# B, C and y of the last two batches turned in 32x32 squares on VectorE, in place of 128x128 transposes on TensorE

## The chip, the cores and the metric

The kernel runs on one core of a Trainium2 chip. The metric is the device time of one execution in microseconds (us). PE is TensorE, DVE is VectorE, ACT is ScalarE, POOL is GpSimd, and SP is the engine whose queue issues all transfers between the chip's main memory and SBUF (its on-chip memory). PSUM is where PE writes.

## The reference, cut to what matters

A scan with decay over sequences (4 batches, 8 heads, 768 tokens, head dimension 32, state dimension 16), followed by a mixer over tokens and channels with weights w1 (256x1024) and w2 (1024x256). All in fp32.

```python
# scan, chunk by chunk of 32 tokens, per batch and head
cum = cumsum(log(a));  L = exp(cum_i - cum_j) for i >= j, else 0
y = (C @ B.T * L) @ x  +  (C @ state) * exp(cum)
state = exp(sum(log a)) * state + sum_j B_j x_j * exp(cum_last - cum_j)

# mixer on x = y as (batch, 768 tokens, 256 channels)
h = x.T @ U @ V               # U (768, 32), V (32, 768)
u = x + h.T
out = u + relu(u @ w1) @ w2
```

## The kernel before

**Tiles.** A batch's 768 tokens are 6 blocks of 128; the scan works on pairs of blocks, so there are 12 pairs (pair k belongs to batch k // 3, place q = k % 3 in it). For pair k, `load_bc` and `load_x` bring B, C and x with tokens on partitions. `prep` multiplies B and C on DVE by the decay factors F, into the tile BC. `turning` makes the state dimension lie on partitions: four TensorE transposes with the identity (L478) into a PSUM bank "w", from which ACT copies T (B and C turned, L482) and Cm (C turned and masked by head, L488). `gram` (C B^T, L510), `mask` (DVE, tile M), `state` and `update` (the running state, DVE and POOL), `inter` (L630) and `intra` (L655) give y in two PSUM banks, channels on partitions. `yout` copies it to yT by ACT.

**From y to the mixer.** The mixer needs y with channels on partitions (yT), and with tokens on partitions (ytok). `ytokening` makes ytok from yT by four TensorE transposes a pair (L682) and one copy, by ACT in the first two batches and by DVE in the last two. `project` (x^T U) reads ytok, `parted` and `added` add h to yT, `split` makes three parts of u for exact products in three passes, `first`, `second`, `third` and `plain` are the product with w1 and the relu, `down` is the product with w2, to which ytok is added on DVE before it is stored. All these products are at L765.

**Order.** The kernel sets the order of all instructions itself, by a list of words, PLAN, which `follow` walks through. A word is a step and its indices: `B6` loads B and C of pair 6, `X6` its x, `w5` a piece of the weights, `c6` converts the words of a weight piece (loaded as 64-bit numbers) on DVE, ACT and POOL, `R` refines a weight. `P6` is `prep`, `T6` half of `turning` (each pair has it twice; `Q` and `V` are the same in smaller parts for the first pairs), `g6` `gram`, `m6` and `M6` the halves of `mask`, `s6`, `u6`, `i6`, `n6`, `j6`, `y6` state, update, inter, the two parts of intra, and `yout`, `t6` `ytokening`. With a batch first: `p`, `q`, `a`, `S` are `project`, `parted`, `added`, `split`; `f`, `e`, `h` and `U` are first, second, third and plain; `d` is a part of `down`. `F` and `E` put matmuls of the identity on PE, so and so many blocks of 128 columns, as fillers ahead of a step that waits.

Each engine runs its instructions in the order in which PLAN records them. Loads and stores all go through the SP queue in that order; a load word also waits for the DVE instruction recorded last before it. Every DVE instruction appears under L174, since a helper records them. `settled` is a small DVE copy for which the second part of `intra` waits. The pools: raw tiles "bc" and "x" have 4 buffers each, BC, T and Cm 3, PSUM two banks for each of the tags w, x, z and y.

Of the kernel before, what the change touches and what calls it, by code (L numbers as in the profile page):

```python
# [14 lines left out]
WCOLS = 512  # L15
NWORDS = 15
PLAIN = 2
TAGS = {(2, 1): "yyy", (3, 0): "yyy", (3, 1): "yyy"}


# [11 lines left out]


PLAN = (
    'YB0 F2 A1 YB1 Q0.2 A0 Q0.0 Q0.1 YX0 K0 YB2 YV0 F5 V0.0.0 V0.1.1 F1 g0 Q1.2 Q1.1 s0 V1.1.2 YX1 '
    'Q1.0 V1.0.2 m0 M0 n0 YX2 F3 g1 Q2.0 Q2.2 u0 YU0 M1 Q2.1 i0 j0 y0 s1 F1 V2.0.2 m1 n1 w0 u1 '
    'V2.1.3 c0 c0 c0 E3 i1 g2 m2 YB3 w1 M2 E4 j1 y1 s2 B5 v0 O0.0 w4 u2 c2 t1 i2 P3 X3 c2 B4 w2 c2 '
    'n2 j2 T3 c1 c1 y2 T3 O2.1 X4 p0 P5 g3 m3 M3 q0 T5 T5 n3 a0.1 a0.0 B6 c1 s3 U0.1.0 P4 w3 U0.1.1 '
    'u3 T4 T4 U0.0.1 i3 c5 c5 c3 g4 X5 j3 c5 c3 w5 s4 U0.0.0 m4 R3 U0.1.6 c3 y3 U0.1.2 P6 U0.0.6 M4 '
    'T6 u4 T6 B7 i4 g5 c4 c4 n4 w6 s5 j4 y4 R1 M5 U0.0.7 c4 U0.1.3 m5 U0.1.7 U0.0.5 R3 c6 u5 U0.0.3 '  # L40
    'P7 T7 w8 n5 R0 i5 c7 R2 X6 c6 g6 w7 j5 c6 y5 T7 U0.1.5 t5 M6 U0.0.2 X9 B10 c7 t3 m6 R2 t4 R1 '
    'c8 U0.0.4 c8 p1 U0.1.4 c7 B8 q1 R4 X7 c8 d0.0.2.0 c9 d0.0.1.0 c9 d0.0.1.1 c9 d0.0.2.1 d0.0.2.2 '
    'd0.0.2.3 d0.1.0.0 a1.0 d0.1.0.1 P8 d0.1.0.2 S1.0 a1.1 R7 d0.0.1.2 d0.0.1.3 d0.1.0.3 s6 g7 m7 '
    'M7 n6 R0 f1.0.0 u6 R6 f1.0.1 f1.0.4 e1.0.0 h1.0.0 f1.0.5 e1.0.4 e1.0.1 f1.0.6 h1.0.4 i6 s7 j6 '
    'h1.0.1 d0.0.0.0 e1.0.5 R4 h1.0.5 f1.0.7 X8 e1.0.6 h1.0.6 d0.0.0.1 d0.0.0.2 e1.0.7 h1.0.7 '
    'f1.0.3 R5 f1.0.2 B9 u7 d0.1.1.0 X10 d0.0.0.3 P10 e1.0.2 R5 y6 h1.0.2 S1.1 e1.0.3 d0.1.2.0 '
    'd0.1.1.1 d0.1.1.2 h1.0.3 d0.1.2.1 d0.1.2.2 T8 T8 d0.1.2.3 d0.1.1.3 n7 s8 u8 i7 g8 j7 P9 s9 '
    'f1.1.0 m8 y7 R7 f1.1.1 d1.0.1.0 M8 e1.1.0 u9 d1.0.0.0 i8 n8 h1.1.0 s10 j8 d1.0.1.1 d1.0.1.2 R6 '
    'd1.0.1.3 R4 R5 u10 d1.0.0.1 d1.0.0.2 d1.0.1.4 e1.1.1 d1.0.0.3 R7 d1.0.2.0 R6 d1.0.2.1 d1.0.2.2 '
    'B11 d1.0.2.3 d1.0.0.4 d1.0.0.5 d1.0.1.5 d1.0.2.4 T10 h1.1.1 f1.1.6 f1.1.7 d1.0.2.5 e1.1.6 '  # L50
    'e1.1.7 f1.1.2 h1.1.6 h1.1.7 f1.1.3 f1.1.4 f1.1.5 X11 e1.1.2 e1.1.4 h1.1.2 h1.1.4 e1.1.3 h1.1.3 '
    'e1.1.5 P11 h1.1.5 T9 T9 d1.1.0.0 d1.1.0.1 d1.1.2.0 d1.1.2.1 d1.1.0.2 d1.1.2.2 d1.1.0.3 y8 t6 '
    'd1.1.2.3 d1.1.1.0 d1.1.1.1 d1.1.1.2 d1.1.1.3 d1.1.2.4 d1.1.0.4 d1.1.0.5 t7 d1.1.1.4 d1.1.1.5 '
    'd1.1.2.5 T10 t8 g9 p2 m9 M9 i9 g10 m10 q2 T11 T11 M10 n9 a2.0 s11 u11 j9 g11 i10 n10 y9 m11 '
    'S2.0 M11 t9 f2.0.0 f2.0.4 f2.0.1 e2.0.0 h2.0.0 e2.0.4 f2.0.5 e2.0.1 h2.0.4 h2.0.1 f2.0.6 '
    'e2.0.5 h2.0.5 f2.0.2 f2.0.3 j10 y10 e2.0.2 e2.0.3 f2.0.7 h2.0.2 h2.0.3 i11 n11 a2.1 e2.0.6 '
    'e2.0.7 j11 h2.0.6 d2.0.0.0 S2.1 y11 d2.0.1.0 d2.0.1.1 d2.0.0.1 f2.1.0 h2.0.7 d2.0.1.2 t11 t10 '
    'e2.1.0 h2.1.0 d2.0.1.3 d2.0.0.2 d2.0.0.3 f2.1.2 d2.0.1.4 d2.0.0.4 d2.0.0.5 d2.0.1.5 f2.1.3 '
    'd2.0.2.0 e2.1.2 h2.1.2 e2.1.3 d2.0.2.1 p3 d2.0.2.2 f2.1.1 f2.1.4 h2.1.3 d2.0.2.3 e2.1.1 f2.1.5 '
    'h2.1.1 e2.1.4 h2.1.4 d2.0.2.4 e2.1.5 q3 d2.0.2.5 h2.1.5 f2.1.6 f2.1.7 a3.0 e2.1.6 e2.1.7 '  # L60
    'h2.1.6 d2.1.2.0 d2.1.2.1 a3.1 d2.1.0.0 d2.1.0.1 d2.1.2.2 d2.1.0.2 S3.0 f3.0.3 f3.0.2 h2.1.7 '
    'd2.1.2.3 d2.1.0.3 f3.0.1 e3.0.2 h3.0.2 d2.1.0.4 e3.0.3 d2.1.0.5 h3.0.3 f3.0.0 e3.0.1 d2.1.1.0 '
    'd2.1.1.1 d2.1.1.2 e3.0.0 h3.0.0 f3.0.5 f3.0.4 d2.1.1.3 f3.0.6 e3.0.4 d2.1.2.4 e3.0.5 h3.0.1 '
    'f3.0.7 h3.0.4 d2.1.2.5 d2.1.1.4 e3.0.6 e3.0.7 d2.1.1.5 d3.0.2.0 d3.0.2.1 h3.0.6 d3.0.2.2 '
    'd3.0.0.0 d3.0.0.1 d3.0.0.2 S3.1 f3.1.0 f3.1.4 f3.1.5 h3.0.7 h3.0.5 d3.0.2.3 e3.1.0 f3.1.1 '
    'h3.1.0 d3.0.0.3 e3.1.4 f3.1.2 e3.1.5 d3.0.0.4 d3.0.0.5 d3.0.2.4 d3.0.2.5 d3.0.1.0 h3.1.4 '
    'd3.0.1.1 h3.1.5 e3.1.1 f3.1.6 f3.1.3 h3.1.1 d3.0.1.2 e3.1.2 e3.1.3 d3.0.1.3 h3.1.2 h3.1.3 '
    'f3.1.7 e3.1.6 h3.1.6 d3.0.1.4 d3.0.1.5 e3.1.7 d3.1.2.0 d3.1.2.1 h3.1.7 d3.1.2.2 d3.1.2.3 '
    'd3.1.1.0 d3.1.1.1 d3.1.2.4 d3.1.2.5 d3.1.1.2 d3.1.1.3 d3.1.0.0 d3.1.0.1 d3.1.0.2 d3.1.0.3 '
    'd3.1.1.4 d3.1.1.5 d3.1.0.4 d3.1.0.5 ')  # L70


@with_exitstack
def kernel(
# [42 lines left out]
    Q = 32  # L117
# [71 lines left out]
            "g r s -> r g s"))  # L189

    x_sb, bc_sb = {}, {}
    pairs = [(b, q) for b in range(NB) for q in range(NPR)]

    def hold(load, until):
# [10 lines left out]

    def load_bc(k, blocks=(0, 1)):
        b, q = pairs[k]
        if k not in bc_sb:
            bc_sb[k] = raw.tile([P, NH, 2, 2, N], FP32, tag="bc", name="bc")
        for c in blocks:  # L210
            begin(
                out=bc_sb[k][:, :, 0, c],
                in_=B[b, :, ts(2 * q + c, P), :].rearrange("h s n -> s h n"))
            if c == 0:
                begin(
                    out=bc_sb[k][:, :, 1].rearrange("p h t n -> p h (t n)"),
                    in_=C[b, :, ts(q, 2 * P), :].rearrange("h (p t) n -> p h (t n)", t=2))

    def load_x(k, blocks=(0, 1)):
        b, q = pairs[k]  # L220
# [70 lines left out]
            load_words(n + 1, w2c(n - NQ - 1, FP32), w22[m * P:(m + 2) * P].rearrange(  # L291
                "(m p) d -> p m d", p=P))

    loads = dict(B=load_bc, X=load_x, w=load_w)
    early = dict(loads, V=lambda n: load_v(), U=lambda n: load_u())

    ident = const.tile([P, P], FP32)
# [55 lines left out]
                            axis=mybir.AxisListType.X, op=ALU.add)  # L353

    F = const.tile([P, NB, NPR, NH, 2, 2], FP32)
    kept = const.tile([P, NB, 2 * NC - 1], FP32)
    own2 = const.tile([P, NB, 2 * NC - 1, 2], FP32)

# [6 lines left out]
    def decays(bs, tag="w", which=range(2)):  # L365

        n = bs.stop - bs.start
        for i in which:
            d = bank(tag, n * NPR * NH * 2)
            view = d.rearrange("p (g h c) -> p c g h", g=n * NPR, h=NH)  # L370
            logs = la[:, bs].rearrange("p b (q c) h -> p c (b q) h", q=NPR)
            if i == 0:
                nc.tensor.matmul(out=view, lhsT=ref, rhs=logs, start=True, stop=True,
                                 skip_group_check=True)
            for c in range(2 if i else 0):
                for t in range(2):
                    nc.tensor.matmul(
                        out=view[ts(c, H), t], lhsT=ref.rearrange("p (i t) -> p t i", t=2)[:, t],
                        rhs=logs[:, c], start=t == 0, stop=True, skip_group_check=True)
            nc.scalar.activation(  # L380
                F[:, bs, :, :, i].rearrange("p b q h c -> p (b q h) c"),
                d.rearrange("p (g c) -> p g c", c=2), AF.Exp, scale=(-1.0, 1.0)[i])

    def keep(bs, tag="w"):

# [61 lines left out]
        yield  # L447


    st = {}  # L450
    settled = const.tile([P, 1], FP32)
    behind = {"turn": 0, "first": []}
    yT, ytok = {}, {}
# [1 line left out]
    def prep(k, c=0, n=2):  # L455

        b, q = pairs[k]
        if "BC" not in st.setdefault(k, {}):
            st[k]["BC"] = att.tile([P, 2, 2, NH, N], FP32, tag="BC", name="BC", bufs=3)
        for g in [slice(4) if n == 2 else slice(c, c + 1) if c < 2 else slice(2, 4)]:  # L460
# [2 lines left out]
                out=part, in0=bc_sb[k].rearrange("p h i c n -> p (i c) h n")[:, g],  # L463
                in1=F[:, b, q].rearrange("p h i c -> p (i c) h")[:, g, :, None].to_broadcast(
                    part.shape), op=ALU.mult)

    def turning(k, c=0, n=2, tag="w", engine=None):

# [33 lines left out]
    def gram(k, tags="xxzz"):  # L502
# [3 lines left out]
        for c in range(2):  # L506
            for p in range(2):
                for r in range(4):
                    rows, cols = ts(r, Q), ts(p, H)
                    nc.tensor.matmul(  # L510
                        out=g[r][cols, c], lhsT=s["T"][rows, 0, c, cols],
                        rhs=s["Cm"][rows, :, :, ts(2 * c + p, Q)].rearrange("r v t i -> r v i t"),
                        start=(c == 0), stop=True,
                        skip_group_check=True)

# [101 lines left out]
    def inter(k):  # L617
# [7 lines left out]
        for c in range(2):  # L625
            for p in range(2):
                own = st.get(("Sm", b, 4 * q + 2 * c + p))
                assert own is not None or 4 * q + 2 * c + p == 0
                for r in range(4 if own is not None else 0):
                    behind["first"].append(nc.tensor.matmul(  # L630
                        out=y[r // 2][ts(r % 2, H), c, p], lhsT=own[ts(r, Q)],
                        rhs=s["T"][ts(r, Q), 1, :, ts(2 * c + p, Q)].rearrange("r t i -> r i t"),
                        start=fresh(k, r // 2, range(2 * (r % 2), 2 * (r % 2) + 2)),
                        stop=True, skip_group_check=True))

# [40 lines left out]
    def ytokening(k, tag="w", copies=None):  # L676

        b, q = pairs[k]
        t = bank(tag, 2, 2, P)
        for c in range(2):  # L680
            for g in range(2):
# [193 lines left out]

    def turned(k):

        t = turns.setdefault(k, turning(k))
        for _ in range(2):
            next(t)  # L880

# [6 lines left out]
    def ytokens_of(k, v):  # L888
# [3 lines left out]
                 M=lambda k: mask(k, (2, 3)), u=update, i=inter, n=lambda k: intra(k, 0),  # L892
                 j=crossed, y=yout, t=ytokens, Q=lambda k, c: prep(k, c, 1),
                 O=ytokens_of,
                 V=lambda k, c, v: turn(k, c, 1, "wx"[v // 2], vector if v % 2 else None))
    whole = dict(c=convert, R=refined, A=lambda i: decays(every_batch, "w", [i]),
                 K=lambda n: keep(every_batch, "z"), F=fill, E=warm,
                 v=lambda n: spread())

    def follow(plan):  # L900

        for word in plan.split():
            name, rest = (word[:2], word[2:]) if word[0] in "YZ" else (word[0], word[1:])
# [51 lines left out]
```

## Time and profile before

| what | value |
|---|---|
| median of 3 runs | 225.64 us (225.54 to 225.82) |
| profiled execution | 225.44 us; its span 223.7 us |
| PE busy | 214.8 us (96%), 3024 matmuls, granted clock 0.999 |
| DVE / ACT / POOL busy | 146.7 / 107.9 / 33.8 us |
| DMA queue of SP | 69488 packets, 14.13 MB, 32.3% of 16 engines' span |
| TensorE transposes of B and C (L478) / of y (L682) | 48 / 48 |
| transfers issued: B 24, C 12, x 24, weights 14, a 1, stores 24 | 99 |

The span is what the profile covers, from the first instruction to the last; the execution's time holds a little more. Busy time of PE counts overlapped matmuls once, and an engine that is busy is not thereby at its best speed.

### The profile page before, as it was taken

To read this page: it belongs to the slowest core of one execution; us is meant where nothing else is said; L and a number is where in the kernel's file an instruction comes from. 1 tells how busy PE (TensorE), PEld (TensorE's weight loads), DVE (VectorE), ACT (ScalarE), POOL (GpSimd) and SP (SyncE) were. 2 spreads that over 40 slices of the span, in tenths; PEclk is the share of its full clock that TensorE was granted. 3 is DMA by queue.
4 is the path that set the end of the run, shared out by engine and by line. 5 is a ranking of instruction groups with operands and counts; after the bars stand their busy time and mean duration, and the time that the engine had idled before them with its cause. 6 is when DMAs were issued, how large, how long until landed. Compare 5 with 4: busy or idle time off the path is not lost.

```text
span 223.7 us, 7032 instructions
## 1 busy us (share of the span) xinstructions
PE 214.8 (96%) x3024; PEld 182.1 (81%) x3024; DVE 146.7 (66%) x311; ACT 107.9 (48%) x250; POOL 33.8 (15%) x43
## 2 busy tenths in 40 slices
PE   7878999999999999999999999999999999999994
PEld 4645655666668888887999997797999999999993
DVE  4867779927853866759636737978825966484821
ACT  3334746575781354461425624577336555554510
POOL 3012301642834020223400000000000000000000
PEclk9999999999999999999999999999999999999999
DMA  6968889962973010461032301000010000101011
GB/s 81 142 105 151 172 134 175 231 139 84 196 97 52 26 50 0 61 107 50 7 47 70 50 22 53 3 3 3 0 50 0 25 3 23 38 8 50 1 50 47
DMA packets 69520, 14.59 MB, mean 65 GB/s; under 512 B 63792, under 2 KB 67696, under 8 KB 69488
## 3 DMA queue, kind: packets, MB, share of 16 engines
q1 hardware_dynamic: 69488, 14.13, 32.3%
q8 instruction: 24, 0.39, 0.8%
q14 instruction: 8, 0.07, 0.1%
HBM read 10.98 MB, written 3.15 MB: 63 GB/s over the span
## 4 chain that ended last, share of the span: by engine, by line
PE 88%; SPq 5%; DVE 3%; DMA 1%; issue 1%; ACT 1%
PE x L765 31%; PE z L765 23%; PE y L765 12%; SPq L202 5%; PE y L655 3%; PE y L630 3%; PE w L682 2%; PE x L510 2%; PE w L545 2%; DMA x<-in_x_dram 1%; PE w L478 1%; DVE M L174 1%; PE z L510 1%; PE w L709 1%; PE x L737 1%; PE w L136 1%
## 5 line engine op out<-in xcount | busy, mean ns | idle before, releaser
L765 PE MATMUL x<-u,w 128*128 128x384 f32 x144 | 32.8, 344 | 0.2 <-DVE M L174 0.2
L765 PE MATMUL z<-u,w 128*128 128x384 f32 x144 | 32.6, 342 | 0.0
L174 DVE SCALAR_TENSOR_TENSOR words<-words 128x768 fp32r<-128x768 f32 (+3 forms) x34 | 30.1, 887 | 1.6
L770 ACT ACTIVATE x<-x 128x384 f32<-128x384 f32 (+1 forms) x30 | 13.6, 454 | 28.4 <-PE x L765 28.4
L765 PEld LDWEIGHTS z<-u,w 128*128 128x128 f32 x144 | 24.9, 188 | 0.6 <-DVE M L174 0.2
L765 PEld LDWEIGHTS x<-u,w 128*128 128x128 f32 x144 | 24.4, 188 | 1.0 <-issue 0.3
L765 PE MATMUL x<-w2c,words 128*128 128x256 f32 x112 | 22.9, 341 | 0.0
L174 DVE SCALAR_TENSOR_TENSOR words<-x,words 128x384 fp32r<-128x384 f32 x24 | 13.1, 554 | 14.8 <-ACT words L799 12.9
L572 POOL TENSOR_TENSOR Sm<-S,own 128x256 f32<-128x256 f32 (+1 forms) x12 | 8.1, 676 | 84.9 <-DVE S L174 47.5
L765 PEld LDWEIGHTS x<-w2c,words 128*128 128x128 f32 x112 | 18.2, 189 | 1.6
L765 PE MATMUL y<-w,words 128*128 128x256 f32 x144 | 19.3, 282 | 0.0
L770 ACT ACTIVATE z<-z 128x384 f32<-128x384 f32 (+1 forms) x27 | 12.5, 465 | 13.0 <-PE z L765 12.6
L765 PEld LDWEIGHTS y<-w,words 128*128 128x128 f32 x144 | 18.7, 190 | 0.0
L174 DVE SCALAR_TENSOR_TENSOR words<-z,words 128x384 fp32r<-128x384 f32 x24 | 13.2, 551 | 5.4 <-ACT words L799 5.4
L799 ACT ACTIVATE words<-z 128x384 fp32r<-128x384 f32 x24 | 11.7, 492 | 9.9 <-PE z L765 9.7
L799 ACT ACTIVATE words<-x 128x384 fp32r<-128x384 f32 x24 | 11.6, 491 | 7.8 <-PE x L765 7.8
L765 PE MATMUL x<-w,words 128*128 128x256 f32 x96 | 13.8, 286 | 0.0
L174 DVE SCALAR_TENSOR_TENSOR S<-S,kept,w 128x64 f32<-128x64 f32 x40 | 11.2, 279 | 2.8 <-PE w L545 1.2
L174 DVE TENSOR_TENSOR ytok<-x,ytok 128x256 f32<-128x256 f32 x10 | 4.2, 423 | 13.2 <-PE x L765 13.2
L655 PE MATMUL y<-M,x 64*32 64x64 f32 x768 | 12.0, 223 | 0.9 <-DVE settled L174 0.9
L765 PEld LDWEIGHTS x<-w,words 128*128 128x128 f32 x96 | 12.5, 190 | 0.3 <-issue 0.2
L655 PEld LDWEIGHTS y<-M,x 64*32 64x32 f32 x768 | 7.8, 105 | 5.8 <-DVE settled L174 1.9
(150 smaller groups left out, 409.7 us busy)
## 6 DMA issues: line engine op xcount, KB each, us to landing
words<-in_moe_w_ch_dram SPq DMA_DIRECT2D x7, 512.0 KB, 4.9
x<-in_x_dram SPq DMA_DIRECT2D x24, 128.0 KB, 3.5
out_dram<-ytok SPq DMA_DIRECT2D x24, 128.0 KB, 1.7
bc<-in_B_dram SPq DMA_DIRECT2D x24, 64.0 KB, 2.9
bc<-in_C_dram SPq DMA_DIRECT2D x12, 128.0 KB, 3.1
words<-in_moe_w_ch_dram SPq DMA_DIRECT2D x2, 256.0 KB, 3.8
words<-in_moe_V_dram SPq DMA_DIRECT2D x4, 48.0 KB, 3.4
words<-in_moe_U_dram SPq DMA_DIRECT2D x1, 192.0 KB, 3.4
```

The costliest lines, as they stand in the source:

```text
L136: nc.tensor.matmul(out=t[:, :m * P].rearrange("p (m i) -> p m i", i=P), lhsT=ident, rhs=ident[:, None, :].to_broadcast([P, m, P]), start=T ...
L174: self.last = call(*args, **kwargs)
L202: op = issuer[0].dma_start(**kwargs)
L510: nc.tensor.matmul(out=g[r][cols, c], lhsT=s["T"][rows, 0, c, cols], rhs=s["Cm"][rows, :, :, ts(2 * c + p, Q)].rearrange("r v t i -> r v i ...
L545: nc.tensor.matmul(out=s["A"][p][ts(r, Q), v], lhsT=s["BC"][half, 0, v, 2 * r:2 * r + 2].rearrange("p h n -> p (h n)"), rhs=x_sb[k][half, ...
L572: nc.gpsimd.tensor_tensor(out=s["Sm"][:, sl], in0=s["S"][:, sl].rearrange("p i (s d) -> p i s d", s=2), in1=own2[:, b, 4 * q + sl.start:4 ...
L630: behind["first"].append(nc.tensor.matmul(out=y[r // 2][ts(r % 2, H), c, p], lhsT=own[ts(r, Q)], rhs=s["T"][ts(r, Q), 1, :, ts(2 * c + p, ...
L655: product = nc.tensor.matmul(out=y[n][ts(i, Q), c, p], lhsT=x_sb[k][half, c, h], rhs=s["M"][half, h // 2, c, h % 2], start=fresh(k, n, [i] ...
L682: nc.tensor.transpose(out=t[:, c, g], in_=yT[b][:, g, ts(2 * q + c, P)], identity=ident)
L765: nc.tensor.matmul(out=t, lhsT=lhsT, rhs=rhs, start=start, stop=True, skip_group_check=True)
L770: nc.scalar.activation(t, t, AF.Copy, scale=1.0 + EPS)
L799: nc.scalar.activation(gs[j, m // 2][0][:, m % 2], t, AF.Relu, scale=NEAR)
```

## The change

It concerns the pairs 6 to 11, the last two batches.

- `load_bc` brings B and C in eight transfers of 32 KB: for B and C, for the even and the odd heads (v) and for each block (c), with four heads times 32 on the partitions, and on each partition four tokens in a row (64 numbers, 256 bytes). The matrix in question is then in squares of 32x32 that stand on the partitions where their turned form has to be.
- `prep` multiplies all of that tile in place by factors in the same layout, Fq. They come from a new step `D` (`squared`): 16 matmuls and two exponentials on ACT.
- `squares` takes the place of `turning`: two DVE transposes (each 32x32 square by itself) write T from the tile, and ACT makes Cm from T. There is no PSUM bank in it.
- `state` still needs B with tokens on partitions. A new load word `L` (`load_plain`, two transfers) brings B a second time into BC, and a new step `N` (`plainly`) multiplies it on DVE into the other half.
- `ytokening` for batches 2 and 3 turns yT with two DVE transposes into a tile of the tag "bc", and 16 transfers from SBUF to SBUF, issued by SP, move the squares to their partitions in ytok.
- `gram` and `inter` read T and Cm of these pairs with tokens in order (`tokens_of`).
- PLAN is another order from the first word on, with the words D, L and N; fillers F are 5 2 6 4 and E 5, where F was 2 5 1 3 1 and E 3 4.

```diff
+SQUARES = 6
+MOVED = 2
...
     def load_bc(k, blocks=(0, 1)):
         b, q = pairs[k]
+        if k >= SQUARES:
+            bc_sb[k] = t = raw.tile([P, 2, 2, 2, 4, N], FP32, tag="bc", name="bc")
+            for i, src in enumerate((B, C)):
+                for v in range(2):
+                    for c in range(2):
+                        begin(
+                            out=t[:, i, v, c].rearrange("p r n -> p (r n)"),
+                            in_=src[b, v::2, ts(2 * q + c, P), :].rearrange(
+                                "g (s r) n -> g s (r n)", r=4))
+            return
...
+    def load_plain(k):
+        b, q = pairs[k]
+        both = st[k]["BC"] = att.tile([P, 2, 2, NH, N], FP32, tag="BC", name="BC", bufs=3)
+        for c in range(2):
+            begin(
+                out=both[:, 1, c],
+                in_=B[b, :, ts(2 * q + c, P), :].rearrange("h s n -> s h n"))
...
+    def squared():
+
+        n = (NB - SQUARES // NPR) * NPR
+        d = bank("w", n, 16)
+        for r in range(4):
+            for g in range(4):
+                nc.tensor.matmul(
+                    out=d[ts(g, Q)].rearrange("p k (v c r) -> p r k c v", v=2, c=2)[:, r],
+                    lhsT=ref.rearrange("p (s r) -> p r s", r=4)[:, r],
+                    rhs=la[:, SQUARES // NPR:, :, 2 * g:2 * g + 2].rearrange(
+                        "p b (q c) v -> p (b q) c v", c=2),
+                    start=True, stop=True, skip_group_check=True)
+        for i in range(2):
+            nc.scalar.activation(Fq[:, :, i], d, AF.Exp, scale=(-1.0, 1.0)[i])
...
     def prep(k, c=0, n=2):
+        if k >= SQUARES:
+            t = bc_sb[k].rearrange("p i v c r n -> p (i v c r) n")
+            vector.tensor_tensor(
+                out=t, in0=t, in1=Fq[:, k - SQUARES // NPR * NPR].rearrange("p i e -> p (i e)")[
+                    :, :, None].to_broadcast(t.shape), op=ALU.mult)
+            return
...
+    def squares(k):
+
+        s = st[k]
+        T = s["T"] = att.tile([P, 2, 2, P], FP32, tag="T", name="T", bufs=3)
+        for i in range(2):
+            vector.transpose(
+                out=T[:, i].rearrange("p c (s r) -> p c r s", r=4),
+                in_=bc_sb[k][:, i].rearrange("p v c r n -> p (c r) v n"))
+        yield
+        yield
+        s["Cm"] = att.tile([P, 2, 2, P], FP32, tag="Cm", name="Cm", bufs=3)
+        for v in range(2):
+            nc.scalar.activation(s["Cm"][:, v], T[:, 1], AF.Copy, scale=slot[:, v, None])
+        yield
+        yield
...
     def ytokening(k, tag="w", copies=None):
+        if b >= MOVED:
+            t = raw.tile([P, 4, 2, 2, Q], FP32, tag="bc", name="bc")
+            for n in range(2):
+                vector.transpose(
+                    out=t[:, :, :, n].rearrange("p m c d -> p c m d"),
+                    in_=yT[b][:, n, ts(q, 2 * P)])
+            for m in range(4):
+                for a in range(4):
+                    nc.sync.dma_start(
+                        out=ytok[b][ts(m, Q), 2 * q:2 * q + 2].rearrange(
+                            "t c (n a d) -> a t (c n) d", n=2, a=4)[a],
+                        in_=t[ts(a, Q), m].rearrange("t c n d -> t (c n) d"))
+            yield
+            return
```

The words of PLAN that the prediction speaks of, after the change, from the start (the first line) and around the last pairs:

```
A1 YB0 YX2 A0 Q0.0 Q0.2 YB1 K0 YX0 YX1 YB2 F5 V0.0.0 w4 Q0.1 ... YU0 ... YV0 g1 m1 YB3 n0 s1 ... w0 M1 ... u1 V2.1.3 w1 B6 B5 X3 B4
... X4 m2 c0 F4 v0 w2 B7 O0.0 P3 c1 t1 n2 c2 i2 c2 T3 c5 j2 c5 y2 X5 T3 D0 O2.1 p0 g3 P5 c1 c1 m3 M3 T5 q0 c2 w3 w5 T5 n3 a0.1 s3
... d1.0.2.5 e1.1.6 t8 ... T11 N10 ... s10 ... g9 m9 p2 ... y9 ... t9 ... t10 ... t11 f2.1.0 ... d2.0.2.3 p3
```

## The prediction

> **What bounds the kernel now.** I read the page's first two parts, then the chain of waits in order of time, then the timelines of the SP queue and of DVE where that chain leaves PE, and last the windows by stage. The page, with busy time by engine and the two slice rows that matter:
>
> ```profile
> PE 214.8 (96%) x3024; PEld 182.1 (81%) x3024; DVE 146.7 (66%) x311; ACT 107.9 (48%) x250; POOL 33.8 (15%) x43
> ...
> PE   7878999999999999999999999999999999999994
> ...
> DMA  6968889962973010461032301000010000101011
> ```
>
> TensorE is busy 96% of 223.7 us, at full clock, and its slices fall under nine tenths only in the first 22 us and at the very end. DMA is the reverse: full for the first 50 us, nearly empty after 70. So there are two regimes: early, loads decide; later, every TensorE instruction taken out is time saved, if nothing new is late. The chain prices the instructions (start, length, engine, line):
>
> ```profile
> 19.97 1.06 PE w L136 x2
> ...
> 45.38 0.44 PE w L478 x4
> ...
> 128.19 0.44 PE w L682 x4
> ```
>
> L478 is the four transposes that turn a pair's B and C, L682 the four that turn its y. Each group of four puts 0.44 us on the path, 0.11 us a transpose. (The groups' mean of 276 ns is the length of overlapped instructions, not their spacing.) L136 is a filler of four blocks, 0.265 us a block.
>
> For the loads I read the SP queue and DVE around 24 us:
>
> ```profile
> 21.54 1.16 SPq L202 DMA_DIRECT2D bc<-in_B_dram  x1
> 22.75 0.57 SPq L202 DMA_DIRECT2D bc<-in_C_dram  x1
> 23.38 0.79 SPq L202 DMA_DIRECT2D bc<-in_B_dram  x1
> 24.26 1.07 SPq L202 DMA_DIRECT2D words<-in_moe_w_ch_dram  x1
> ```
> ```profile
> 24.15 0.49 DVE L174 TENSOR_SCALAR words<-words 128x256 f32<-128x256 f32 x2 [0.50 <-DMA words<-in_moe_w_ch_dram]
> ```
> ```profile
> 20.00:30.00 10.00, 8.92 (x247) 5.18 (x248) 6.93 (x20) 5.78 (x17) 3.01 (x4) 1.00 0.85 154
> 30.00:40.00 10.00, 9.93 (x211) 6.51 (x211) 9.22 (x24) 5.56 (x12) 1.60 (x2) 1.00 0.90 163
> ```
>
> DVE stands idle for a load at 24 us (bracket), and the last two columns of the windows show DMA engines 0.85 and 0.90 busy. A load put ahead of others here is paid for, unless a row shows slack. And the store's issue, for the price of one small transfer on the SP queue (min/median/max ns):
>
> ```profile
> L834 SPq DMA_DIRECT2D out_dram<-ytok x24: 332/333/524, 72.0 to 221.0; - x24
> ```
>
> **The change, part by part.** The profiled execution took 225.44 us, 1.74 around its span of 223.7, and 0.2 under the median of the runs (225.64). The sum is made against 225.44, and 0.2 is added at the end.
>
> Removed from TensorE: six pairs (6 to 11) times two groups of four transposes, 12 x 0.44 = 5.3 us. These stand after 60 us, where PE is at nine tenths or more, so all of it is path. The Trainium skill, page "VectorE: DVE Perf Modes", section "The three transpose paths", gives 390 ns for a 128x128 bf16 transpose on TensorE and 311 ns for VectorE's 32x32 blocks. By that figure, as an estimate, the twelve groups would be 48 x 0.39 = 18.7 us and the time near 211; the chain's 0.11 us contradicts it, and the sum goes by the chain.
>
> Added on TensorE: D, 16 small matmuls of 24 columns with 128 partitions in and 32 out. Nearest row: the four matmuls of L377 (96 columns) from 4.74 to 5.23 us, 0.12 each. By columns 16 x 0.03 = 0.5, at the same price each 1.9; I take 0.8, nearer the columns. Fillers go from 19 blocks (F 12, E 7) to 22 (F 17, E 5): 3 x 0.265 = 0.8 if paid, nothing where PE waits anyway; I take 0.5. TensorE's net is -4.0 us.
>
> ACT loses the six copies of T (592 ns each) and keeps the two Cm per pair, now from SBUF; at 48% busy that counts nothing. DVE gains per pair: two transposes of 256 columns for B and C, two for y, one product for the plain B (N), and loses the y copy (688 ns). No row shows a DVE transpose: bounds are the 128x128 product (285 ns) and twice the 128x256 product (2 x 420 ns); I take 0.42. So 5 x 0.42 - 0.69 = 1.4 us a pair, 8.5 in all, and DVE goes from 147 to 155 of some 222 us. In the stages where it lands (100 to 165 us) DVE is 45 to 88% busy, so it is covered; with the upper bound it adds 10 us more, and the masks and halves queued behind each transpose could make PE wait some tenths each time, up to 2 us.
>
> Loads, moved and added: pairs 6 to 11 get eight transfers of 32 KB for B and C where there were three, and two more for the plain B: 60 where there were 18. Nothing is late for that after 60 us, where DMA is at 0.1 to 0.3 for long stretches. What matters is the new order early. Ahead of pair 5's B and C now come, besides what came before, w4 (512 KB) and the eight transfers of pair 6. w4 also passes w0 and w1, and w1 is the load for which DVE stood idle above, with the copy "settled" behind it on DVE and the next intra product on PE behind that (it waited 0.34 us). So w4 delays there by its engine time: 512 KB at the 230 GB/s of the busiest early slices is 2.2 us, at the least the 1.07 us of its issue; I take 1.5. Pair 5 then waits further: its B and C landed at 26.5 us and DVE took them at 28.47, 2 us of slack; its product stands on DVE ahead of pair 3's masks, and PE's T5, n3 and a0.1 stand behind. Eight issues at 0.333 + 0.04 between them are 3.0 us, so pair 5 is late by 1.5 + 3.0 - 2 = 2.5, of which 1.5 is the same shift as w4's and about 1.2 us is new PE work ahead of T5: 0 to 0.5 remains. The early stage therefore costs +2.0 us (range 1 to 4).
>
> y's moves: 16 transfers a pair, 128 pieces of 128 bytes each, 16 x 0.373 = 6.0 us of SP queue and 1.7 us from issue to landing (the stores' median). Pairs 6 and 7 go together, 32 x 0.373 = 12 us; behind them stand three stores, pair 8's moves and x of pair 11, none needed for 13 us or more. The tight place is pair 11 before p3. Between t11 and p3 PE has five f (0.70), four e (0.35) and eight parts of d (0.47): 8.7 us. Needed: the split of u ahead on DVE partly, 0.84 for the two transposes, 6.0 and 1.7: 8.5 plus what DVE lags. I book +0.3 (0 to 2).
>
> Sum: -5.3 + 0.8 + 0.5 + 2.0 + 0.3 = -1.7 us; 225.44 - 1.7 + 0.2 = **223.9 us**.
>
> **Rivals.** First, nothing early is late: the fillers and the earlier x loads (x of pair 1 ended PE's wait at 16.2 us; now 13th instead of 18th in the queue) absorb w4. Then -5.3 + 0.8 = -4.5 and less for fillers: 221.3 to 222.5, say 221.6. Against it: the idle bracket above leaves no slack.
>
> Second, on the slow side: the eight small transfers of a pair don't spread over the 16 DMA engines, because their source is cut first into four heads, then 32 rows. A packet costs 0.323 x 16 x 223.7 us / 69488 = 16.6 ns on its engine. Spread over 16, a pair's 1024 packets are 1.1 us; on four engines 256 x 16.6 = 4.25 us, and any load behind them that uses all engines ends with the slowest four. Ahead of w5 now stand pairs 6 and 7, where pair 6 alone stood (3072 packets, 3.2 us): 2 x 4.25 - 3.2 = 5.3 us later. w5 landed at about 45.5 us in before, its three DVE steps take 1.9, and in the new order j4's "settled" stands right behind them; it ran at 47.6, so there is no slack but the 1.8 us by which the steps ahead of j4 have grown. Stall 3.5 us at 16.6 ns a packet, and with 256 bytes in a packet it can be more: at 25 ns 2 x 6.4 - 3.2 - 1.8 = 7.8. The times are 225.64 - 4.0 + 0.3 plus these, 225.4 to 229.7, say 227.5. It decides from 4.0 us of stall, 17.6 ns a packet. For it: DMA at 0.85 to 0.9 until 48 us. Against it: no transfer of before has so short a first dimension, so no row shows such a spread. The Trainium skill, page "DMA: Bandwidth & Descriptors", section "Why a DMA increments its semaphore by 16 and not by 1", says that a transfer uses the largest number of engines up to 16 that divides the slowest dimension of both sides, which here is four. By that rule the spread of this rival is certain and only its price is open; no trace here shows it yet.
>
> Third, the moves are late at p3: if one costs 0.57 us on SP (as the C loads), pairs 9 to 11 need 48 x 0.57 + 1.7 = 29 us, where PE's steps between t9 and p3, at the prices above, come to 22.5: a stall of up to 6.5 in place of 0.3, 226 to 230, say 228. Against it: the stores, with as many pieces, take 0.333.
>
> Fourth, the second rival at its lowest price: the gain is just used up, 225.4 to 225.9.
>
> **Chances.** Forecast 0.40 (its own range 222.6 to 225.1), first rival 0.12, second 0.28, third 0.12, fourth 0.08. The second gets much, since its condition is in the code, but its price must be above the mean packet's. The range of 221.3 to 228.4 takes in forecast, first rival and most of the second and third. Under 0.2% (0.45 us) a measurement can't tell this kernel from no change. Faster: 0.40 less a tail of 0.03, plus 0.12, 0.49. Same: 0.08 and bits of the tails, 0.09. Slower: 0.42.
>
> **What would show it.** Right: the groups of L478 and L682 fall from 48 to 24 each; PE busy near 211; PE idle in 20 to 40 us up by about 2 us, behind DVE products of bc and words that wait for DMA; no wait on DMA ahead of p3's matmuls (line 805 of the new file); the 96 small moves near 0.35 us each. Wrong: early stalls of 5 us or more with eight-transfer loads landing after 4 us or more; PE waiting for ytok's DMA before p2 or p3; DVE transposes over 0.8 us; or a PE that is idle less than before in the first 40 us.

## The result, and the profile after

The changed kernel takes 254.93 us (median of 4 runs, 252.50 to 255.98) against 225.73 for the kernel before on the same chip: ratio 1.126, 95% interval 1.120 to 1.131. The forecast was 223.9 us, in a range of 221.3 to 228.4. The profiled execution took 254.47 us, its span is 252.8. The page, same rows as before and the clock:

```profile
PE 222.0 (88%) x3008; PEld 184.6 (73%) x3008; DVE 152.1 (60%) x337; ACT 106.1 (42%) x246; POOL 31.5 (12%) x43
...
PE   6986989999999999999979808999990699999994
...
PEclk9996899999999999999999965599999599999999
DMA  6995695957413244303111314011111100010001
```

PE has two holes, near 145 and near 193 us, that were not there before, and a weaker start. Behind each of the three places the granted clock falls (the 6 and the 5s), and PE is busy for 7 us more although it has 16 instructions less (the run below with GpSimd's copies and an earlier filler has as many, a clock of 1.00 throughout, and PE busy for 214.8 us). DMA is nearly empty in both holes. The chain of waits by engine (SPq is SP's queue):

```profile
PE 62%; SPq 15%; DVE 10%; ACT 5%; issue 3%; DMA 2%; POOL 0%; DVEq 0%; POOLq 0%
```

Before, 88% of it was PE. 15% of 252.8 us are 38 us, and the chain by line gives them all to L761, the y moves. The line of the moves (min/median/max ns), the SP queue in time (start, length), and PE at the two holes (last bracket: idle time and who ended it):

```profile
L761 SPq DMA_DIRECT2D ytok<-bc x96: 585/599/1983, 116.2 to 196.3; - x96
```
```profile
116.19 22.23 SPq L761 DMA_DIRECT2D ytok<-bc  x32
138.53 1.51 SPq L922 DMA_DIRECT2D out_dram<-ytok  x3
140.13 10.72 SPq L761 DMA_DIRECT2D ytok<-bc  x16
...
163.89 33.05 SPq L761 DMA_DIRECT2D ytok<-bc  x48
```
```profile
152.41 0.66 PE L805 MATMUL w<-ytok,UV 128*32 128x128 f32 x8 [7.83 <-DMA ytok<-bc]
```
```profile
198.24 0.66 PE L805 MATMUL w<-ytok,UV 128*32 128x128 f32 x8 [8.52 <-DMA ytok<-bc]
```

A move occupies SP for 0.60 us, with 0.04 to the next. Six pairs are 96 x 0.64 = 61 us of a queue, half of which has to be through before p2 and the rest before p3. Pair 8's moves stand behind those of 6 and 7 and three stores, pair 11's behind those of 9 and 10, and the last third of p2 (8 of its 24 matmuls) and of p3 waits 7.8 and 8.5 us. The windows by stage (columns: stretch, length, busy time with counts of PE, PE's weight loads, DVE, ACT, POOL, then granted clock, DMA share, GB/s):

```profile
20.00:30.00 10.00, 7.44 (x161) 4.27 (x154) 5.61 (x19) 2.08 (x7) 2.08 (x3) 0.66 0.58 112
30.00:40.00 10.00, 9.07 (x260) 6.13 (x259) 6.63 (x18) 7.04 (x21) 1.44 (x2) 1.00 0.81 146
140.00:150.00 10.00, 4.58 (x96) 3.97 (x94) 2.69 (x7) 0.92 (x3) 0.00 (x0) 0.86 0.22 49
150.00:160.00 10.00, 7.09 (x182) 4.30 (x188) 3.06 (x8) 1.87 (x5) 0.00 (x0) 0.50 0.33 74
190.00:200.00 10.00, 1.76 (x12) 1.38 (x13) 0.16 (x1) 0.44 (x2) 0.00 (x0) 0.75 0.20 46
```

In the early stretch PE does 1.5 us less in 20 to 30 us than before, at a clock of 0.66, with the DMA engines less busy (0.58) than before (0.85). So loads are not what is short there. The loss by stage, with the starts of the first U product, of p1's first and p2's and p3's last matmul (us):

| kernel | U0.1.0 | p1 | p2 | p3 | end of span |
|---|---|---|---|---|---|
| before | 33.2 | 63.2 | 136.7 | 167.8 | 223.7 |
| after | 39.8 | 71.2 | 152.6 | 198.5 | 252.8 |
| y by TensorE, new order | 39.0 | 70.4 | 145.8 | 181.7 | 234.5 |
| order alone | 39.2 | 75.2 | 154.6 | 190.6 | 243.5 |
| the same as the third, E5 ahead of s2 | 36.0 | 68.5 | 145.4 | 181.3 | 234.2 |
| moves by GpSimd, new order | 41.2 | 72.6 | 144.1 | 178.8 | 231.7 |
| moves by GpSimd, E5 ahead of s2 | 35.7 | 68.3 | 139.8 | 174.5 | 227.5 |
| old order, B and C in squares | 34.3 | 64.4 | 152.0 | 185.3 | 241.2 |
| old order, y in squares, GpSimd, t6 late | 33.6 | 63.6 | 136.0 | 168.5 | 224.5 |

Of the 29.1 us, 8.0 lie ahead of p1 and 21.1 behind it. (The new order does one U block of 1.3 us more ahead of p1, and some 3.4 us more of the mixer ahead of p3.) The changed kernel and its versions with two queues, longer runs and GpSimd's copies have the same program up to p1, and their profiles put U0.1.0 at 39.8, 39.0, 41.5 and 41.2 us: a difference of 2 us there tells nothing by itself.

### The profile page after: what moved, and what is told of

Same layout as the page of the kernel before. It is cut to its first block, busy times and chain, and to the rows that moved or that the text cites. A ratio compares the mean times of both kernels' runs of the same rounds, so it can differ in the third digit from the quotient of the medians.

```text
span 252.8 us, 7206 instructions
## 1 busy us (share of the span) xinstructions
PE 222.0 (88%) x3008; PEld 184.6 (73%) x3008; DVE 152.1 (60%) x337; ACT 106.1 (42%) x246; POOL 31.5 (12%) x43
## 4 chain that ended last, share of the span: by engine, by line
PE 62%; SPq 15%; DVE 10%; ACT 5%; issue 3%; DMA 2%; POOL 0%; DVEq 0%; POOLq 0%
PE x L853 20%; SPq L761 15%; PE z L853 15%; PE y L853 11%; DVE words L176 4%; PE x L584 3%; DMA ytok<-bc 2%; PE y L704 2%; PE w L138 2%; DVE M L176 2%; PE y L729 2%; DVE S L176 1%; ACT words L887 1%; ACT z L858 1%; PE w L815 1%
## 5 line engine op out<-in xcount | busy, mean ns | idle before, releaser
L853 PE MATMUL x<-u,w 128*128 128x384 f32 x144 | 34.1, 356 | 1.9 <-DVE words L176 1.7
L853 PE MATMUL z<-u,w 128*128 128x384 f32 x144 | 33.3, 349 | 0.1
L853 PEld LDWEIGHTS x<-u,w 128*128 128x128 f32 x144 | 26.1, 198 | 3.4 <-DVE words L176 2.3
L853 PEld LDWEIGHTS x<-w2c,words 128*128 128x128 f32 x112 | 18.9, 199 | 2.2 <-issue 0.4
L805 PE MATMUL w<-ytok,UV 128*32 128x128 f32 x48 | 2.6, 326 | 16.3 <-DMA ytok<-bc 16.3
L176 DVE TENSOR_TENSOR M<-z,causal 128x256 int32<-128x256 int32 x24 | 9.0, 414 | 11.5 <-PE z L584 11.5
L747 ACT COPY yT<-y 128x256 f32<-128x256 f32 x24 | 7.8, 381 | 18.4 <-PE y L729 18.4
L729 PE MATMUL y<-M,x 64*32 64x64 f32 x768 | 12.7, 237 | 1.7 <-DVE settled L176 1.3
L729 PEld LDWEIGHTS y<-M,x 64*32 64x32 f32 x768 | 8.4, 114 | 8.0 <-issue 2.9
```

The source lines that it names most:

```text
L176: self.last = call(*args, **kwargs)
L729: product = nc.tensor.matmul(out=y[n][ts(i, Q), c, p], lhsT=x_sb[k][half, c, h], rhs=s["M"][half, h // 2, c, h % 2], start=fresh(k, n, [i] ...
L747: nc.scalar.copy(out=yT[b][:, n, ts(q, 2 * P)], in_=st[k]["y"][n].rearrange("p c v i -> p (c v i)"))
L805: nc.tensor.matmul(out=p[ts(to, Q), ts(half, P)], lhsT=U_sb[:, c + v], rhs=ytok[b][:, c + v, ts(half, P)], start=to not in seen, stop=True ...
L853: nc.tensor.matmul(out=t, lhsT=lhsT, rhs=rhs, start=start, stop=True, skip_group_check=True)
```

## The experiments

Theory A: the loss behind p1 is the issue of the moves. Theory C: the early loss is the new order's; its rival D: the four-engine loads' (the second rival of the prediction). The other theories are named in the expectation ahead of each run. In code, "..." marks what is left out.

### The moves: y by TensorE, by two queues, in longer runs, by GpSimd

```diff
-MOVED = 2
+MOVED = 4
 # PLAN: t7, t6 behind u9; t9 behind u11
```

> The changed kernel with y turned by TensorE again for all batches (no moves on chip; t6 and t7 placed behind u9 and t9 behind u11, where a PSUM bank is free). Theory A (the loss behind p1 is the issue of the y moves on SP at 0.6 us each, and the low clock that follows PE's waits for them): the waits for ytok before p2 and p3 and DVE's wait for the buffer go; from p1 to the end it takes about 158 us (before: 160.4, less some 6 groups of B and C transposes at 0.44), p1 stays near 71, so the time is about 231 us. Theory B (the loads on four engines and the DVE transposes of B and C delay the scan's second half as well): p1 to the end stays over 168 us, the time is 240 us or more.

Measured: 237.22 us, ratio 1.047 (1.042 to 1.052). From p1 to the end 164.1 us, where after has 181.6 and before 160.5. Both waits for ytok are gone, so A holds for 17 of the 21 us. The time itself is 6 us over A's figure: p2 to p3 takes 35.9 us, partly work that this order does earlier, and the transposes put back wait 2.4 us at 121 us for a bank "w".

```diff
-                    nc.sync.dma_start(
+                    (nc.sync, nc.scalar)[a % 2].dma_start(
```

> The changed kernel with the y moves issued by SP and ACT in turn. Theory A1 (0.6 us is what one queue needs for one issue): 16 moves take about 5.2 us on each queue side by side instead of 10.3, the wait before p2 falls from 7.8 us to under 3 and the one before p3 from 8.5 to under 3, ACT's copies and splits are held by 8 x 0.6 per pair; time about 240 us. Theory A2 (the 0.6 us lie in something both queues share): the last move of a batch ends as late as before, the waits stay, time about 254 us or more.

Measured: 274.12 us, ratio 1.214 (1.206 to 1.221). The queues are separate, as A1 has it: 32 moves took 12.6 us instead of 22.2. But ACT stood still meanwhile. Its timeline:

```profile
115.95 12.00 ACTq L761 DMA_DIRECT2D ytok<-bc  x16
128.00 0.37 ACT L858 ACTIVATE x<-x 128x256 f32<-128x256 f32 x1 [11.79 <-DMA ytok<-bc]
```

The scaling of a `down` product waited 11.8 us behind 16 issues, and PE with it. A1's mechanism was right and its time wrong by 34 us: I had named ACT's delay (8 x 0.6 us a pair) and not asked what waits for ACT.

```diff
-                            "t c (n a d) -> a t (c n) d", n=2, a=4)[a],
-                        in_=t[ts(a, Q), m].rearrange("t c n d -> t (c n) d"))
+                            "t c (h e) -> t (c h) e", h=2)[:, a],
+                        in_=t[ts(a, Q), m].rearrange("t c n d -> t (c n d)"))
```

> The changed kernel with each y move as 32 contiguous pieces of 512 bytes instead of 128 pieces of 128 bytes; same count of transfers, same bytes; the squares land in other columns, so y of batches 2 and 3 is permuted in ytok. Theory A3 (the price of a move is set by its pieces): a move takes 0.35 us or less on SP, the waits before p2 and p3 nearly go, time 232 to 238 us. Theory A4 (it is a price for the transfer): a move still takes 0.58 to 0.64 us, 16 take 10 us, time 252 to 256 us.

Measured: 253.48 us, ratio 1.118 (1.112 to 1.124), and the moves:

```profile
L761 SPq DMA_DIRECT2D ytok<-bc x96: 508/589/1626, 118.4 to 199.1; - x96
```

A quarter of the pieces, the same 0.59 us: it is a price for the transfer (A4), not for its pieces. The bytes were not changed here; the changed kernel's loads of 32, 128 and 512 KB from main memory have medians of 0.53, 0.58 and 0.63 us on the same queue, so they too matter little.

```diff
-                    nc.sync.dma_start(
+                    nc.gpsimd.tensor_copy(
```

> The changed kernel with the 96 y moves as copies of 32 partitions x 128 by GpSimd instead of transfers from SP. Theory A (the moves' issue is what costs behind p1): at 0.2 to 0.35 us a copy a pair needs 3 to 6 us and no landing time, the waits before p2 and p3 shrink to under 2 us each, time 233 to 240 us. Theory B (turning y by DVE at all, with the second step behind it, is too late for p2 and p3): waits of over 4 us stay before p2 and p3, time over 245 us.

Measured: 232.99 us, ratio 1.027 (1.021 to 1.033). A copy took 0.29 us, 16 took 5.9 to 7.2, and no matmul of p2 or p3 waited for one. So the same squares, in the same order, with another carrier, are 22 us faster. That is A. From p1 to the end it is 159.1 us, 1.4 under before, which is no more than the U block of 1.3 us that this order does ahead of p1: with the waits gone, the twelve groups of transposes that PE no longer does still don't show as a gain.

```profile
L761 POOL COPY ytok<-bc x96: 281/290/1099, 117.6 to 176.0; 32x128 f32<-32x128 f32 x96
```

### The early stretch: the order alone, the filler, w4

```diff
-SQUARES = 6
-MOVED = 2
+SQUARES = 12      # B, C loaded and turned as before; D, L, N do nothing
+MOVED = 4         # t6, t7, t9 as above; four transposes at the second T
```

> The changed kernel's order alone: B, C and y of all pairs turned by TensorE as before, B and C loaded over all 128 partitions as before (D, L and N do nothing; t6, t7, t9 placed as in the run with y on TensorE; a pair's four TensorE transposes stand together at its second T). Theory C (the early 6.5 us come from the order: w4 ahead of w0 and w1, later F, V and c words): U0.1.0 starts near 39 us and p1 near 70 as in the changed kernel, time about 232 us. Theory D (they come from the four-engine loads of pairs 6 to 8, 24 transfers of 0.6 us on SP, which hold SP's queue and four DMA engines): U0.1.0 is back near 34 us, p1 near 64, time about 226 us.

Measured: 246.03 us, ratio 1.088 (1.082 to 1.093). U0.1.0 starts at 39.2 us with loads over all 128 partitions, as with loads on four engines (39.0). So the first 6 us are the order's, its fillers included (C), and D falls for them. The time is 14 us over C's figure. My putting a pair's four transposes in one place costs some of it: behind 50 us PE stands 2.6 us ahead of a product into a bank "w" and runs at 0.66 in 60 to 65 us. This run does not tell what the order alone costs behind U0.1.0.

```diff
-... c0 n1 s2 c0 E5 i1 u2 ...
+... c0 n1 E5 s2 c0 i1 u2 ...
```

> The run with y on TensorE in the new order (237.2 us), with one word moved: the five filler blocks E5 stand ahead of s2 instead of behind it. Theory F (E5 takes a w bank that s2 has just filled, so PE waits for u2 and POOL's Sm behind it, idles at 20 to 22.5 us and then runs at half clock): the wait of PE for S at 22 us and the clock of 0.5 to 0.8 in 20 to 30 us go, U0.1.0 comes 3 to 5 us earlier (39 to about 35), time 232 to 234.5 us. Theory G (the words and masks on DVE are late anyway): PE waits as long somewhere else before 30 us, time 236.5 to 238 us.

Measured: 235.76 us, ratio 1.039 (1.034 to 1.045), 1.5 us under the run it starts from. U0.1.0 comes 3.0 us earlier. The filler E5 takes a bank "w"; both were held by s2's products until u2 on DVE, which had weight words ahead of it. So the filler that was to keep PE's clock up made PE wait 2.6 us and run at a low clock. The same window without that:

```profile
20.00:30.00 10.00, 9.29 (x302) 6.16 (x300) 7.54 (x25) 6.32 (x19) 2.02 (x3) 1.00 0.50 101
```

PE 9.29 of 10 us, clock 1.00, where the changed kernel has 7.44 and 0.66. Theory F's mechanism holds. Its time, 234.5 us at most, was not reached: by p2 the lead of 3.0 us has shrunk to 0.4, and no run shows why. With the moves on GpSimd as well (both edits above):

> The run with the moves on GpSimd in the new order (233.0 us) with E5 ahead of s2. Theory F (the filler behind s2 costs about 3 us at U0.1.0, of which 1.5 reached the end in the run with y on TensorE): U0.1.0 near 37 us, time 230.5 to 232 us. Otherwise 233 us.

Measured: 229.71 us, ratio 1.018 (1.015 to 1.021), granted clock 1.000 throughout; a little better than F had it. Here the lead stays to the end. Against before, 5.1 us are left at p1 (68.3 against 63.2); behind p1 the two take 159.2 and 160.5 us.

```diff
-... V0.0.0 w4 Q0.1 ... v0 w2 ...
+... V0.0.0 Q0.1 ... v0 w4 w2 ...
```

> The run with the copies on GpSimd and E5 ahead of s2 (229.7 us), with w4 moved from ahead of w0 and w1 to behind v0. By the prediction's term w4 ahead of w0 and w1 costs 2.0 us: U0.1.0 near 35 instead of 37.1, time about 228 us. If the early stretch is bound by the words on VectorE and ScalarE and not by loads: U0.1.0 stays at 36.5 to 37.5, time 229 to 230.5 us.

Measured: 241.26 us, ratio 1.067 (1.063 to 1.071), U0.1.0 only at 48.8 us. A miss of both expectations: the new order also converts w4 early (the first c5 is ahead of y2), so DVE stood 12.4 us for the load, which in SP's queue was behind pair 6's eight transfers and those of pairs 5 and 4. Neither expectation is decided; w4 belongs early in this order.

### B and C alone, in the old order

```diff
 # PLAN of before; SQUARES = 6, MOVED = 4
+... B6 L6 ... P6 N6 ... T5 T5 D0 ...     # L behind B, N behind P, pairs 6 to 11
```

> B and C of the last two batches in squares as in the changed kernel, y by TensorE, in the word order of before (L behind B, N behind P, D behind the second T5). Theory C (the early loss is the new order's): the first stretch is as before, U0.1.0 near 33 us, p1 near 63; PE is spared six groups of four transposes, 6 x 0.44 = 2.6 us, less 0.8 for D; time about 224 us (222.5 to 226). Theory D (the loads on four engines delay whoever waits for B and C): p1 later than 66 us, time 229 us or more.

Measured: 244.27 us, ratio 1.078 (1.070 to 1.086). The start is nearly that of before (p1 at 64.4), as C has it and against D, but the time is 18 us over C's range. In SP's queue and on DVE:

```profile
71.49 2.26 SPq L206 DMA_DIRECT2D bc<-in_C_dram  x4
79.30 1.00 SPq L206 DMA_DIRECT2D BC<-in_B_dram  x2
```
```profile
82.48 0.42 DVE L177 TENSOR_TENSOR BC<-BC,F 128x256 f32<-128x256 f32 x1 [6.01 <-DMA BC<-in_B_dram]
```

L7 waits in SP's queue from 73.8 to 79.3 us until a buffer of BC is free, and N7 waits for it in DVE's queue, with all that stands behind it there. Before, BC was filled by DVE alone and no load could do that.

The same with y in squares as well, copied by GpSimd (MOVED = 2):

> The word order of before, B and C of the last two batches in squares, y of these batches in squares with the moves as GpSimd copies. If order and moves were the whole loss: p1 near 63 us, p2 and p3 wait for the last copies of t8 and t11, which stand close ahead of them, up to 4 us each; time 222 to 230 us. If the squares themselves cost time (DVE's 1.05 us per pair for B and C and 0.84 for y, ACT's Cm from SBUF): 232 us or more.

Measured: 262.11 us, ratio 1.156 (1.150 to 1.160): the same wait, and 13.0 us of PE at p2 and p3 for GpSimd's copies, which stand too close ahead of them in the old order. Both parts of its expectation came together, larger than I had them.

```diff
-... B6 L6 ... P6 N6 ...
+... s4 L6 ... p1 N6 ...     # L7 s5, L8 s6, L9 s7, L10 u8, L11 s9; N: a1.0 s7 P9 u9 P11
```

> The order of before with B and C of the last two batches in squares and y by TensorE, as in the run that took 244.3 us, but the plain copies of B are loaded only once the buffer they go to is free (L6 behind s4, L7 behind s5, L8 behind s6, L9 behind s7, L10 behind u8, L11 behind s9) and N comes late (behind p1, a1.0, s7, P9, u9, P11). Theory L (the 18 us were the plain loads waiting in SP's queue for their buffer, with the loads behind them): DVE's wait of 6.0 us for BC goes, time 223 to 227 us. Theory D (four-engine loads, or squares by DVE, are slow wherever they stand): 232 us or more.

Measured: 233.94 us, ratio 1.036 (1.033 to 1.039). The wait for BC is gone, and 10 of the 18 us with it, so L explains over half; the time itself lies in D's range. Of the 9.6 us that are left in the profiles, 5.8 lie between p1 and p2: pair 8's DVE transposes start only at 102.8 us, behind the splits and halves recorded ahead of them, PE waits 1.5 us for their Cm, and the clock is 0.66 in 105 to 115 us. D, in the form that squares by DVE come late in a queue that is full, is not refuted (DVE is busy for 9.6 of the 10 us from 100 us on). That B and C in squares can gain anywhere is not shown by any run.

### y alone, in the old order, and a hybrid

y of batches 2 and 3 in squares, GpSimd's copies, B and C by TensorE (SQUARES = 12, PLAN of before with t6 behind y7):

> One part alone in the word order of before: only y of the last two batches is turned by VectorE, its squares copied by GpSimd (0.37 us a copy in the run with the moves on GpSimd, 5.9 us a pair); B and C as before; t6 stands behind y7, t7 behind u10, t8 to t11 each behind their y. Theory A (without the transfers from SP the y part is a gain): PE is spared 6 x 0.44 = 2.6 us, p2 and p3 wait under 1 us for the last copies; time 222.5 to 225 us. Rival H (three pairs need 18 us of GpSimd ahead of p2 and of p3, which is too late in this order): waits of 2 to 5 us before p2 and p3 and a lower clock behind them, time 228 to 236 us.

Measured: 234.41 us, ratio 1.037 (1.035 to 1.039). The time is in H's range, but not for H's reason (no wait at p2): t6's copies, 5.2 us on GpSimd, stood ahead of weight work there, for which ACT, DVE and then PE waited in turn:

```profile
116.12 0.68 PE L729 MATMUL y<-M,x 64*32 64x64 f32 x32 [6.67 <-DVE settled L177]
```

Then t6 and t7 behind the last R6:

> The run with y alone in the order of before (234.4 us), with t6 and t7 placed behind the last of the weights' words on GpSimd (R6) and t8 behind y8. Theory I (there 5.2 us of copies stood in GpSimd's queue ahead of weight work that PE waited for, 6.7 us): that wait goes, p2 waits 0 to 3 us for t8's copies instead; time 224 to 229 us. If the copies cost by the squares or the order in another way: 232 us or more.

Measured: 226.26 us against 226.23, ratio 1.002 (1.000 to 1.004). Theory I holds; the loss is gone, but so is the gain of 2.6 us.

```diff
+            for m in range(4):
+                for a in range(4):
+                    vector.transpose(out=ytok[b][ts(m, Q), ...], in_=yT[b][ts(a, Q), ...])
```

> As the run with y alone in the order of before, but the second step is left out: 16 VectorE transposes of 32 x 128 per pair write each square straight to the partitions it belongs to, with no GpSimd copy and no transfer. If VectorE takes 0.1 to 0.2 us each, a pair costs it 1.6 to 3.2 us instead of 0.84, nothing waits before p2 and p3, time 222.5 to 225 us; if 0.3 us or more each (4.8 us a pair), masks and splits come late, time 227 us or more.

Measured: 254.93 us, ratio 1.131 (1.125 to 1.136). A VectorE transpose of 32 x 128 took 0.30 us, nearly as long as those of 128 x 256 (0.42), and 16 of them hold DVE's queue 5 us a pair; PE waited up to 6.6 us for masks behind them.

```diff
-        if b >= MOVED:
+        if b == MOVED:
```

> The run with y alone (226.26 us), with batch 2 alone in squares and batch 3 by TensorE as before. Theory J (between p1 and p2 PE is the bound and keeps what is spared; between p2 and p3 it waits for the scan, and transposes there fill its waits): p1 to p2 stays 1.0 us shorter than before, p2 to p3 is 31.1 us again, time 0.6 to 1.0 us under the kernel before. Rival: level with it within 0.3 us.

and, with all of y in squares again, `... M11 t9 ... a2.1 t10 ... d2.0.1.2 t11 ...`:

> The run with y alone (226.26 us), with t9 behind M11, t10 behind a2.1 and t11 behind d2.0.1.2, so that VectorE's transposes of batch 3 stand behind the scan's masks and updates instead of among them. If they stood in the scan's way: p2 to p3 falls to about 30 us unless p3 waits for t11's copies (5.9 us behind its transposes, with some 8 us of PE work between), time 224.5 to 225.5 us. By theory J: p2 to p3 stays at 31 to 32.5 us, time 225.5 to 227 us.

Measured: batch 2 alone 225.95 us, ratio 0.996 (0.993 to 0.9995); with late t9 to t11 229.13 us, ratio 1.012 (1.008 to 1.015). The window from 150 us bears on why batch 3's transposes were worth nothing. In turn: before, all y in squares, batch 2 alone:

```profile
150.00:160.00 10.00, 9.75 (x181) 8.60 (x180) 8.84 (x15) 5.47 (x13) 0.00 (x0) 1.00 0.01 2
```
```profile
150.00:160.00 10.00, 8.56 (x169) 7.28 (x169) 8.33 (x17) 5.00 (x12) 5.72 (x13) 1.00 0.01 2
```
```profile
150.00:160.00 10.00, 9.75 (x180) 8.59 (x179) 8.85 (x14) 5.62 (x14) 0.00 (x0) 1.00 0.01 2
```

Without y's transposes PE is idle for 1.2 us more here, and p2 to p3 is not shorter (32.5 us against 31.1; batch 2 alone 31.2), as theory J has it. DVE, at 8.3 to 8.9 of 10 us, carries the scan's masks and updates there. Why p2 to p3 is 1.4 us longer is not shown: late transposes did not help (p2 to p3 34.2 us, of which 1.6 is a wait for t11's copies, and a time over the ranges of both expectations). By its stages batch 2 alone does as J says (p1 to p2 72.4 us against 73.5). Its 0.4% is no proof of a gain: the kernel before took 227.18 us beside it, and 225.7 to 226.4 beside the runs ahead of it.

Last, the order of before up to p1 and the new order's remaining words behind it, all in squares, copies by GpSimd:

> Squares for B, C and y with GpSimd copies; the word order of before up to p1 (D behind the second T5, no new fillers), and behind it the words of the new order that are left. Theory C (the loss left in the run of 229.7 us lies ahead of p1 and is the new order's): p1 near 63.5 to 64.5 us, 159 to 161 us from there (U0.1.4 at 1.3 us now behind p1), time 224.5 to 227 us. If the new order's rest needs what its own start has loaded and converted: loads of B, C and their plain copies come late behind p1, time 230 us or more.

Measured: 237.25 us, ratio 1.049 (1.045 to 1.053); p1 at 63.9 us as expected, but then DVE waits 7.4 and 3.1 us for plain B (L6 goes out at 71.7 us, behind sixteen small loads of B and C and X7) and PE 8.3 us at q1. So the second half of the expectation came true: the new order's rest leans on its own start.

## Why the prediction was wrong, point by point

- **The step that failed is the price of a move, 16 x 0.373 = 6.0 us a pair.** It was read from the stores (0.333 and 0.04 to the next), and measured is 0.64, so 10.2 us a pair. Most stores stand alone in the queue; two that came together in the old trace started 0.45 us apart, and its loads that followed right behind another took 0.57:

```profile
112.77 0.39 SPq L202 DMA_DIRECT2D bc<-in_B_dram  x1
113.21 0.57 SPq L202 DMA_DIRECT2D bc<-in_C_dram  x1
113.84 0.57 SPq L202 DMA_DIRECT2D bc<-in_B_dram  x1
```

  The row I took was the cheapest of its kind and not the one most like the case. The sum's +0.3 for the moves became 22 us (after against the same kernel with GpSimd's copies: 254.9 to 233.0). The same price stands in the early term: eight loads at 3.0 us, which took 4.9.
- **The third rival had the mechanism and the price** (0.57 us a move, a stall at p3) and was given 0.12. It left out p2, where pair 8's moves stand behind 32 others (7.8 us), and the clock, below; 228 us was far too low. The range would not have held even with the moves right: with GpSimd's copies the time is 233.0 us, over its upper end of 228.4, by the early term and TensorE's, below.
- **The early term, +2.0 us for loads** was 6.6 at U0.1.0, and of another cause: the order alone, with the old loads, loses 6.0. Three to 5.5 us go with the filler behind s2 (39.0 to 36.0, and 41.2 to 35.7 with GpSimd's copies). I had costed the fillers by their length (0.5) and not by the PSUM bank that each takes. What the rest is, 2.5 to 2.8 us in which 0.7 of D and 0.8 of filler blocks lie, stays open.
- **The second rival** was half right. Its spread is seen: in two windows with hardly more than pair 6's or pair 7's small loads under way, the DMA share (last column but one) is a quarter.

```profile
24.00:26.00 2.00, 2.00 (x47) 1.42 (x52) 0.00 (x0) 0.00 (x0) 0.24 (x1) 0.50 0.28 61
40.00:42.00 2.00, 2.00 (x7) 1.21 (x7) 1.70 (x6) 0.49 (x1) 0.56 (x1) 1.00 0.25 56
```

  The rule in the Trainium skill, "DMA: Bandwidth & Descriptors", section "Why a DMA increments its semaphore by 16 and not by 1" (engines used divide the slowest dimension), agrees with these 0.25 to 0.28 of 16 engines. But it cost no time that a run shows: eight loads took SP 4.9 us to issue, about as long as four engines need for them at the prediction's 16.6 ns a packet (4.25), and U0.1.0 is no earlier with the old loads.
- **TensorE's -5.3 us for twelve groups** were counted as if all of it were path. Three of them, y of batch 3, lay in waits by theory J; in the run with y alone three others brought 1.1 us from p1 to p2 (predicted 1.3). B and C's six brought nothing that a run shows. PE's busy time, forecast near 211 us, is 214.8 at full clock with GpSimd's copies and E5 ahead of s2, the same as before: the net of -4.0 was not there.
- **DVE transposes**: 0.63 us for T from the load tile and 0.42 for y, where 0.42 was taken with bounds of 0.285 to 0.84. By the Trainium skill, "VectorE: DVE Perf Modes", section "The three transpose paths", VectorE is the faster of the two for a transpose (311 against 390 ns); here a pair's B and C take DVE 1.26 us, and PE 0.44 by the old chain, so for this kernel the measurement speaks the other way.

```profile
L176 DVE STREAM_TRANSPOSE T<-bc 128x256 f32<-128x256 f32 x12 | 6.7, 632 | 0.1
L176 DVE STREAM_TRANSPOSE bc<-yT 128x256 f32<-128x256 f32 x12 | 4.6, 420 | 1.9 <-DMA ytok<-bc 1.9
```

- **D** was right: its 16 matmuls, 32 of 0.22 us each in the trace, overlapped, are 0.7 us busy against 0.8.
- One reading was loose, without weight in the sum: DMA is not nearly empty from 70 us on, since two slices at 89 to 100 us are at 0.4 and 0.6.

## What to carry to other kernels

Price many small transfers by rows in which several are issued back to back, and add up the whole queue to each consumer: here 96 of them cost 22 us, in place of 24 transposes that took TensorE 2.6. When work is moved off the bounding engine, look for what every step then holds (a PSUM bank, a buffer, a place in GpSimd's, ACT's or SP's queue), since most losses that these traces show were an instruction that waited in a queue with urgent work behind it. And count spared time only in stages where that engine does not wait anyway.

## What was not expected of the hardware

- A move of 16 KB from SBUF to SBUF costs its queue 0.59 to 0.60 us with 32 pieces as with 128, while the DMA engines are busy for 0.14 to 0.17 of the time (with 128); two queues issue side by side (32 in 12.6 us).
- The granted clock fell to 0.50 in PE's waits of 2.0, 7.8 and 8.5 us in the changed kernel. Four filler matmuls behind the first took 2.47 us, and the same four 1.35 with E5 ahead of s2. Windows of 0.2 us show when it fell:

```profile
20.80:21.00 0.20, 0.00 (x0) 0.00 (x0) 0.20 (x2) 0.20 (x2) 0.00 (x0) 0.61 0.43 53
147.00:147.20 0.20, 0.00 (x0) 0.00 (x0) 0.00 (x0) 0.00 (x0) 0.00 (x0) 0.84 0.06 11
194.80:195.00 0.20, 0.00 (x0) 0.00 (x0) 0.00 (x0) 0.00 (x0) 0.00 (x0) 0.81 0.00 0
```

  The Trainium skill, "TensorE: Matmul & The Clock Gate", section "What's actually happening", has the clock at half after an idle window of about 3.4 us; the half is borne out, but the time is not the same at each place. It fell 0.3 us into the first wait (PE had been busy for 2.6 of the 3.5 us ahead of it), 2.6 and 5.2 us into the other two, and was back 11.8 and 3.5 us after work began again behind these. With the waits at 16.3 us and PE's wait for a "bc" buffer at 1.5, some 3 of the 21 us behind p1 are left for the clock; that share is worked out and was not measured alone.
- GpSimd copies a square of 32 x 128 to other partitions in 0.29 us (0.37 to 0.45 from one to the next), where the transfer costs its queue 0.60, and with no landing time.
- A VectorE transpose of 32 x 128 takes 0.30 us, one of 128 x 256 with eight times the numbers 0.42.
